# Squared-ReLU MLP: warm-up matmuls as four concurrent column tiles, and the natural-layout weight group kept only in the first block

## The chip, the cores and the metric

The kernel runs on one core of one Trainium2 chip. The metric is device time in microseconds (us) of one execution. A "span" is the time from the first to the last profiled instruction; it is about 1.8 us shorter than the device time of the same execution.

## The reference

```python
# x (1, 2048, 576), w1 (576, 4608), b1 (4608), w2 (4608, 576), b2 (576), all bfloat16
def reference(x, w1, b1, w2, b2):
    h = jnp.einsum("bsd,df->bsf", x, w1) + b1
    r = jnp.where(h > 0, h, 0)
    h = r * r
    return jnp.einsum("bsf,fd->bsd", h, w2) + b2
```

## The kernel before

The 2,048 rows of x are worked through in four blocks of 512. The hidden dimension is cut into 36 "f-tiles" of 128. The contraction of the first product is 576 = 4.5 x 128, an awkward size: nine pieces of 64. The kernel has two ways to deal with it.

- **Row tiles** (32 of the 36 f-tiles): the array is used as two tiles of 64 rows. Each works on its own f-tile, nine matmuls each, and the two run side by side. The weights `w1_h` hold one f-tile's 64-row pieces in the lower half of the partitions and its partner's in the upper half.
- **Natural layout** (the first four f-tiles): four full 128-row matmuls each, and one 64-row piece that is paired with another f-tile's.

The second product runs as full matmuls over 512 output columns, and its remaining 64 columns as two concurrent 64-column tiles (`phase_t`), for two blocks at once.

```python
    WARM = [512] * 6 + [128]
    for i, n in enumerate(WARM):                       # keeps the engine busy until x lands
        keep(nc.tensor.matmul(wps[:, 0:n], lhsT=ones[:, 0:P], rhs=ones[:, 0:n], start=True, stop=True))
    # [...]
    def a_rows(sb, dup_at=None, dup_sb=None):          # row tiles, 16 pairs of f-tiles
        for j in range(NJ):
            # [...]
            for i in range(NC):                        # nine pieces of 64
                keep(nc.tensor.matmul(bx[:], lhsT=w1_h[0:H, LO_C[i], jc], rhs=xT[0:H, LO_W[i], :], ...))
                keep(nc.tensor.matmul(by[:], lhsT=w1_h[H:P, UP_C[i], jc], rhs=xT[H:P, UP_W[i], :], ...))
            evac_h(sb, bx, G + j)
            evac_h(sb, by, G + NJ + j)
    # [...] a_full(sb, order): the natural group, 16 full matmuls and 2 pairs
    for (j0, j1) in [(0, 1), (1, 2), (2, 4), (4, 6), (6, 8), (8, 10), (10, 12)]:
        load_w1(nc.sync, 0, j0, j1)                    # lower half of the partitions
        load_w1(nc.sync, 1, j0, j1)                    # upper half
        # [...]
    load_xT(1)
    for (j0, j1) in [(12, 14), (14, 16)]:
        load_w1(nc.sync, 0, j0, j1)
        load_w1(nc.sync, 1, j0, j1)
    # [...] b2, six loads of w2, further x
    a_full(0, "k_outer")
    a_rows(0, 12, 1)
    a_rows(1)
    a_full(1, "rows_first")
    phase_t(0)
    phase_b(0, hTs[0], dups=(2, 3))
    phase_b(1, hTs[1])
    a_full(2, "g_outer")
    a_rows(2)
    a_rows(3)
    a_full(3, "rows_first")
    phase_t(2)
    # [...]
```

Of the kernel before, what the change touches and what calls it, by code (L numbers as in the profile page):

```python
# [11 lines left out]
BF16 = mybir.dt.bfloat16  # L12
FP32 = mybir.dt.float32
# [4 lines left out]
def kernel(  # L18
# [9 lines left out]
    nc = tc.nc  # L28
    keep = tc.keep_in_program_order
    P = 128  # L30
    H = 64
# [7 lines left out]
    G = 4  # L39
# [18 lines left out]

    wps = ps_o.tile([P, 512], FP32, name="wps", tag="po")
    ones = nc.const_aps.tensor(1.0, [P, 512], BF16)  # L60
    WARM = [512] * 6 + [128]
    for i, n in enumerate(WARM):
        keep(nc.tensor.matmul(wps[:, 0:n], lhsT=ones[:, 0:P], rhs=ones[:, 0:n], start=True, stop=True))  # L63

    xs = const.tile([P, RT, D], BF16, name="x_sb")
    w1n = wpool.tile([P, NK, GW], BF16, name="w1n")
    w1n8 = wpool.tile([P, G // 2, P], BF16, name="w1n8")
    w1_h = wpool.tile([P, NC, FH], BF16, name="w1_h")
    w1_v = w1.rearrange("(c p) f -> p c f", p=H)

    def load_x(eng, rt):
# [9 lines left out]
    def load_w1(eng, h, j0, j1):  # L81
        keep(eng.dma_start(out=w1_h[h * H:(h + 1) * H, :, j0 * P:j1 * P],
                      in_=w1_v[:, :, GW + h * FH + j0 * P:GW + h * FH + j1 * P]))

    load_x(nc.sync, 0)
    load_x(nc.scalar, 1)
# [31 lines left out]
    def dup_windows(sb):  # L118
        xT = xT_blk[sb]
        keep(nc.vector.tensor_copy(out=xT[0:H, SPC:SPC + 4, :], in_=xT[H:P, E3:E3 + 4, :]))  # L120
        keep(nc.vector.tensor_copy(out=xT[H:P, SPC:SPC + 4, :], in_=xT[0:H, O:O + 4, :]))  # L121
# [24 lines left out]
    def x_transpose(j, k):  # L146
        h, q = divmod(j, 2)
        qc = slice(q * P, (q + 1) * P)
        bank, slot, c0 = (half_banks[h][k], 0, k * P) if k < NK else (half_banks[h][2], 1, D - P)
        keep(nc.tensor.transpose(bank[:, slot, qc], xs[:, j, c0:c0 + P], ident[:]))  # L150

    def x_copies(h):
        hc = slice(h * HS, (h + 1) * HS)
        for k in range(NK):
            src = half_banks[h][k][:, 0, :]
            if k % 2 == 0:
                keep(nc.vector.tensor_copy(out=xT0[:, O + k, hc], in_=src))  # L157
            else:
                keep(nc.scalar.copy(out=xT0[:, O + k, hc], in_=src))  # L159
        keep(nc.vector.tensor_copy(out=xT0[:, E3, hc], in_=half_banks[h][2][:, 1, :]))  # L160
# [4 lines left out]
    def make_b1T():  # L165
        b1T_ps = ps_o.tile([P, P], BF16, name="b1T_ps", tag="po")
        keep(nc.tensor.transpose(b1T_ps[:], b1_rows[:], ident[:]))  # L167
        keep(nc.vector.tensor_copy(out=b1T[:], in_=b1T_ps[:, 0:NFT]))
# [6 lines left out]
    def evac_h(sb, bank, ft):  # L175
        r = rpool.tile([P, SB], BF16, name="r", tag="r")
        keep(nc.scalar.activation(out=r[:], in_=bank[:], func=ACT.Relu, bias=b1T[:, ft:ft + 1], scale=1.0))  # L177
        keep(nc.vector.tensor_tensor(out=hTs[sb][:, ft, :], in0=r[:], in1=r[:], op=ALU.mult))  # L178

    def a_rows(sb, dup_at=None, dup_sb=None):  # L180
        xT = xT_blk[sb]
        for j in range(NJ):
            if j == dup_at:
                dup_windows(dup_sb)
            bx = ps_h.tile([P, SB], FP32, name="ph", tag="ph")
            by = ps_h.tile([P, SB], FP32, name="ph", tag="ph")
            jc = slice(j * P, (j + 1) * P)
            for i in range(NC):
                keep(nc.tensor.matmul(bx[:], lhsT=w1_h[0:H, LO_C[i], jc], rhs=xT[0:H, LO_W[i], :],  # L189
                                 start=(i == 0), stop=(i == NC - 1)))  # L190
                keep(nc.tensor.matmul(by[:], lhsT=w1_h[H:P, UP_C[i], jc], rhs=xT[H:P, UP_W[i], :],  # L191
                                 start=(i == 0), stop=(i == NC - 1)))
            evac_h(sb, bx, G + j)
            evac_h(sb, by, G + NJ + j)

    def a_full(sb, order):
        xT = xT_blk[sb]
        banks = []
        for g in range(G):
            pool, tag = (ps_o, "po") if g < 2 else (ps_h, "ph")  # L200
            banks.append(pool.tile([P, SB], FP32, name="pn", tag=tag))

        def pair(i, start, stop):
            keep(nc.tensor.matmul(banks[2 * i][:], lhsT=w1n8[0:H, i, :], rhs=xT[0:H, SPC, :],  # L204
                             start=start, stop=stop, skip_group_check=order == "k_outer"))
            keep(nc.tensor.matmul(banks[2 * i + 1][:], lhsT=w1n8[H:P, i, :], rhs=xT[H:P, E3, :],  # L206
                             start=start, stop=stop, skip_group_check=order == "k_outer"))

        def full(g, k, start, stop):
            keep(nc.tensor.matmul(banks[g][:], lhsT=w1n[:, k, g * P:(g + 1) * P], rhs=xT[:, O + k, :],  # L210
                             start=start, stop=stop))

        if order == "rows_first":
            for i in (1, 0):
                pair(i, True, False)
            for g in (2, 3, 0, 1):
                for k in range(NK):
                    full(g, k, False, k == NK - 1)
                evac_h(sb, banks[g], g)
        else:  # L220
            if order == "k_outer":
                tb_new = [ps_h.tile([P, 2, HS], BF16, name="tb", tag="ph") for _ in range(2)]
                half_banks[1] = tb_new + tb_po

                def part(h, k):
                    hc = slice(h * HS, (h + 1) * HS)
                    for g in range(G):
                        keep(nc.tensor.matmul(banks[g][:, hc], lhsT=w1n[:, k, g * P:(g + 1) * P],  # L228
                                              rhs=xT[:, O + k, hc], start=(h == 0 and k == 0), stop=False,
                                              skip_group_check=True))  # L230

                for j in range(2):
                    for k in range(NK):
                        x_transpose(j, k)
                for j in range(2):
                    x_transpose(j, NK)
                x_copies(0)
                part(0, 0)
                for k in range(NK + 1):
                    x_transpose(2, k)  # L240
                part(0, 1)
                part(0, 2)
                for k in range(NK + 1):
                    x_transpose(3, k)
                x_copies(1)
                dup_windows(0)
                part(0, 3)
                part(1, 0)
                make_b1T()
                for k in range(1, NK):  # L250
                    part(1, k)
            else:
                for g in (2, 3, 0, 1):
                    for k in range(NK):
                        full(g, k, k == 0, False)
            for i in (1, 0):
                pair(i, False, True)
                evac_h(sb, banks[2 * i], 2 * i)
                evac_h(sb, banks[2 * i + 1], 2 * i + 1)

    ft_order = list(range(G))
    for j in range(NJ):
        ft_order += [G + j, G + NJ + j]

    t_order = ft_order[G:] + ft_order[:G]
    EDGES = [0, 384, 512]

    def phase_t(sb):
        pt = ps_o.tile([P, SB], FP32, name="pt", tag="po")
        for i, ft in enumerate(t_order):  # L270
            for h in range(2):
                keep(nc.tensor.matmul(pt[h * DT:(h + 1) * DT, :], lhsT=w2_sb[:, ft, DM:D], rhs=hTs[sb + h][:, ft, :],  # L272
                                      start=(i == 0), stop=(i == NFT - 1)))
        oT = tpool.tile([P, SB], BF16, name="oT", tag="oT")
        keep(nc.scalar.activation(out=oT[:], in_=pt[:], func=ACT.Identity, bias=b2T[:], scale=1.0))  # L275
        ot = tpool.tile([P, RT, P], BF16, name="ot", tag="ot")
        keep(nc.sync.dma_start_transpose(out=ot[:, :, :], in_=oT[:, :]))
        for h in range(2):
            r0 = (sb + h) * SB
            dst = out2[r0:r0 + SB, DM:D].rearrange("(j p) d -> p j d", p=P)  # L280
            keep(nc.sync.dma_start(out=dst, in_=ot[:, :, h * DT:(h + 1) * DT]))
# [20 lines left out]
            load_w1n8(nc.sync, 0)  # L302
            load_w1n8(nc.sync, 1)
    load_xT(1)
    for (j0, j1) in [(12, 14), (14, 16)]:
        load_w1(nc.sync, 0, j0, j1)
        load_w1(nc.sync, 1, j0, j1)
    keep(nc.sync.dma_start(out=b2_bc[:], in_=b2.partition_broadcast(P)))
    for c in (0, 3, 1, 4, 2, 5):
        load_w2(c)  # L310
    load_xT(2)

    alloc_hT(0)
    a_full(0, "k_outer")
    a_rows(0, 12, 1)
    alloc_hT(1)
    load_xT(3)
    a_rows(1)
    a_full(1, "rows_first")
    phase_t(0)  # L320
    phase_b(0, hTs[0], dups=(2, 3))
    phase_b(1, hTs[1])
    alloc_hT(2)
    a_full(2, "g_outer")
    a_rows(2)
    alloc_hT(3)
    a_rows(3)
    a_full(3, "rows_first")
    phase_t(2)
    phase_b(2, hTs[2])  # L330
    phase_b(3, hTs[3], last=True)
# [30 lines left out]
```

## Time and profile before

| | before |
|---|---|
| device time, median of the first 3 runs | 291.73 us |
| span of the profiled run | 289.8 us |
| TensorE busy | 285.1 us (98%) |
| first row pair starts | 9.77 us |
| one slot (row pair, full matmul, or column pair, 512 columns) | 0.216 us |

The kernel is bound by TensorE. The page of the profile says so three times; the lines are its busy table, its chain of work that ended last, and its costliest group.

```profile
PE 285.1 (98%) x2017; PEld 133.7 (46%) x2032; DVE 79.5 (27%) x176; ACT 95.2 (33%) x152; POOL 2.8 (1%) x11
PE 98%; issue 0%; DVE 0%
L191 PE MATMUL ph<-xTw,w_h 64*128 64x512 bf16 x576 | 124.6, 376 | 0.0
```

The last number of the third line is idle time before the group: none. A matmul's mean duration (376 ns) is longer than a slot because consecutive matmuls overlap in the profile; start-to-start times are what count. The next lines are the timeline of TensorE around the end of block 1 (start us, duration us, engine, line, operation, tiles, shape, count).

```profile
72.38 0.38 PE L204 MATMUL pn<-xTw,w1n 64*128 64x512 bf16 x1
72.38 0.38 PE L206 MATMUL pn<-xTw,w1n 64*128 64x512 bf16 x1
72.59 0.38 PE L204 MATMUL pn<-xTw,w1n 64*128 64x512 bf16 x1
72.59 0.38 PE L206 MATMUL pn<-xTw,w1n 64*128 64x512 bf16 x1
73.13 3.40 PE L210 MATMUL pn<-xTw,w1n 128*128 128x512 bf16 x15 [0.16 <-issue]
76.46 7.96 PE L272 MATMUL pt<-hT,w_sb 128*64 128x512 bf16 x72
```

A row pair starts as two lines at the same time. Then comes the natural group (16 matmuls, of which the first is missing from the trace: x15), then the column pairs. Two changes of tiling mode stand here. From the individual starts (in ns: 72,591, then 73,129, with one missing, put 216 earlier) the first takes 0.32 us start to start instead of 0.216; the second 0.31, plus 0.02 in the slot after it.

The last lines are the waits of TensorE, all there are: no matmul waits for a load.

```profile
PE wps L63 <- PEq L346: 0.8, 1, 0.8
PE pn L210 <- issue: 0.3, 2, 0.2
PE po L293 <- issue: 0.3, 2, 0.2
```

### The profile page before, as it was taken

The numbers are of one execution on the slowest core, as the hardware profiler recorded it, in microseconds if no ns is written. First come the engines' busy times: TensorE is split into PE (matmuls) and PEld (weight loads), VectorE is DVE, ScalarE is ACT, GpSimd is POOL, SyncE is SP. The second block draws the span as 40 slices with busy tenths as digits, with TensorE's granted clock in tenths as the row PEclk, the third lists the DMA queues.
The fourth block names the chain that finished last, engine by engine and source line by source line (L and its number), as shares of the span: only waits on it lengthen the run. The fifth ranks groups of instructions, "written<-read, shape, count | busy, mean of one in ns | idle before, by whom it ended". The sixth has DMA issues, their size and how long they took to land.

```text
span 289.8 us, 4679 instructions
## 1 busy us (share of the span) xinstructions
PE 285.1 (98%) x2017; PEld 133.7 (46%) x2032; DVE 79.5 (27%) x176; ACT 95.2 (33%) x152; POOL 2.8 (1%) x11
## 2 busy tenths in 40 slices
PE   8999999999999999999999999999999999999996
PEld 5544444444444444444444444444445444444454
DVE  1644554444502100000025444444440000000001
ACT  2666666666500000000027666666670000000000
POOL 3000000000000000000000000000000000000000
PEclk9999999999999999999999999999999999999999
DMA  7999999400001000000000000000000200000000
GB/s 198 213 235 185 315 388 234 83 0 2 0 19 33 5 20 18 18 18 20 18 18 2 1 2 0 2 0 2 0 2 0 38 18 18 18 20 18 20 18 20
DMA packets 30581, 16.26 MB, mean 56 GB/s; under 512 B 14676, under 2 KB 30560, under 8 KB 30560
## 3 DMA queue, kind: packets, MB, share of 16 engines
q1 hardware_dynamic: 30176, 15.65, 21.7%
q8 instruction: 16, 0.26, 0.4%
q10 hardware_dynamic: 288, 0.30, 0.4%
q14 instruction: 5, 0.04, 0.0%
q0 software_dynamic: 96, 0.01, 0.0%
HBM read 11.36 MB, written 2.36 MB: 47 GB/s over the span
## 4 chain that ended last, share of the span: by engine, by line
PE 98%; issue 0%; DVE 0%
PE po L293 43%; PE ph L189 42%; PE pt L272 5%; PE pn L210 4%; PE pn L228 1%; PE wps L63 1%; PE tb L150 1%; PE ph L191 1%; PE pn L204 1%; DVE o_sb L295 0%; PE b1T_ps L167 0%; PE pn L206 0%
## 5 line engine op out<-in xcount | busy, mean ns | idle before, releaser
L191 PE MATMUL ph<-xTw,w_h 64*128 64x512 bf16 x576 | 124.6, 376 | 0.0
L189 PE MATMUL ph<-xTw,w_h 64*128 64x512 bf16 x576 | 124.6, 376 | 0.0
L293 PE MATMUL po<-w_sb,hT 128*128 128x512 bf16 (+2 forms) x600 | 123.8, 366 | 0.8 <-issue 0.3
L177 ACT ACTIVATE r<-ph,b1T 128x512 bf16<-128x512 f32 x128 | 81.0, 684 | 41.7 <-PE ph L191 41.7
L293 PEld LDWEIGHTS <-hT 128*128 128x128 bf16 x612 | 58.3, 98 | 66.7 <-issue 0.8
L189 PEld LDWEIGHTS <-w_h 64*128 64x128 bf16 x576 | 54.1, 94 | 68.3
L178 DVE TENSOR_TENSOR hT<-r 128x512 bf16<-128x512 bf16 x144 | 61.1, 425 | 75.9 <-ACT r L177 75.4
L191 PEld LDWEIGHTS <-w_h 64*128 64x128 bf16 x576 | 54.1, 94 | 0.0
L295 DVE TENSOR_TENSOR o_sb<-po,b_bc 128x512 bf16<-128x512 f32 (+2 forms) x17 | 11.2, 660 | 125.0 <-PE po L293 125.0
L177 ACT ACTIVATE r<-pn,b1T 128x512 bf16<-128x512 f32 x16 | 10.3, 687 | 68.7 <-PE pn L206 67.4
L272 PE MATMUL pt<-hT,w_sb 128*64 128x512 bf16 x144 | 15.9, 380 | 0.0
L272 PEld LDWEIGHTS <-w_sb 128*64 128x64 bf16 x144 | 8.0, 110 | 7.8 <-issue 0.8
L210 PE MATMUL pn<-xTw,w1n 128*128 128x512 bf16 x45 | 10.4, 379 | 0.4 <-issue 0.3
L210 PEld LDWEIGHTS <-w1n 128*128 128x128 bf16 x48 | 4.5, 98 | 6.0 <-issue 0.8
L275 ACT ACTIVATE oT<-pt,b2T 128x512 bf16<-128x512 f32 x2 | 1.4, 687 | 14.5 <-PE pt L272 14.5
L228 PE MATMUL pn<-xTw,w1n 128*128 128x256 bf16 x32 | 4.8, 304 | 0.0
L228 PEld LDWEIGHTS <-w1n 128*128 128x128 bf16 x32 | 3.4, 110 | 0.6
L63 PE MATMUL wps<-const-bfloat16-1.0 128*128 128x512 bf16 (+1 forms) x7 | 2.8, 581 | 0.8 <-PEq L346 0.8
L157 DVE COPY xTw<-tb 128x256 bf16<-128x256 bf16 x4 | 1.1, 292 | 6.6 <-PE tb L150 6.6
L120 DVE COPY xTw<-xTw 64x2048 bf16<-64x2048 bf16 x4 | 2.8, 690 | 0.2
L121 DVE COPY xTw<-xTw 64x2048 bf16<-64x2048 bf16 x4 | 2.7, 687 | 0.1
L159 ACT COPY xTw<-tb 128x256 bf16<-128x256 bf16 x4 | 1.3, 375 | 3.7 <-PE tb L150 3.7
(23 smaller groups left out, 16.9 us busy)
## 6 DMA issues: line engine op xcount, KB each, us to landing
w_sb<-in_w_dram SPq DMA_DIRECT2D x6, 864.0 KB, 9.6
w_h<-in_w_dram SPq DMA_DIRECT2D x14, 288.0 KB, 6.8
out_dram<-o_sb SPq DMA_DIRECT2D x15, 128.0 KB, 1.7
w_h<-in_w_dram SPq DMA_DIRECT2D x4, 144.0 KB, 3.6
w1n<-in_w_dram SPq DMA_DIRECT2D x4, 128.0 KB, 3.7
x_sb<-in_x_dram ACTq DMA_DIRECT2D x2, 144.0 KB, 2.8
x_sb<-in_x_dram SPq DMA_DIRECT2D x2, 144.0 KB, 3.3
out_dram<-ot SPq DMA_DIRECT2D x4, 64.0 KB, 1.8
```

The costliest lines, as they stand in the source:

```text
L63: keep(nc.tensor.matmul(wps[:, 0:n], lhsT=ones[:, 0:P], rhs=ones[:, 0:n], start=True, stop=True))
L150: keep(nc.tensor.transpose(bank[:, slot, qc], xs[:, j, c0:c0 + P], ident[:]))
L177: keep(nc.scalar.activation(out=r[:], in_=bank[:], func=ACT.Relu, bias=b1T[:, ft:ft + 1], scale=1.0))
L178: keep(nc.vector.tensor_tensor(out=hTs[sb][:, ft, :], in0=r[:], in1=r[:], op=ALU.mult))
L189: keep(nc.tensor.matmul(bx[:], lhsT=w1_h[0:H, LO_C[i], jc], rhs=xT[0:H, LO_W[i], :], start=(i == 0), stop=(i == NC - 1)))
L191: keep(nc.tensor.matmul(by[:], lhsT=w1_h[H:P, UP_C[i], jc], rhs=xT[H:P, UP_W[i], :], start=(i == 0), stop=(i == NC - 1)))
L204: keep(nc.tensor.matmul(banks[2 * i][:], lhsT=w1n8[0:H, i, :], rhs=xT[0:H, SPC, :], start=start, stop=stop, skip_group_check=order == "k_o ...
L210: keep(nc.tensor.matmul(banks[g][:], lhsT=w1n[:, k, g * P:(g + 1) * P], rhs=xT[:, O + k, :], start=start, stop=stop))
L228: keep(nc.tensor.matmul(banks[g][:, hc], lhsT=w1n[:, k, g * P:(g + 1) * P], rhs=xT[:, O + k, hc], start=(h == 0 and k == 0), stop=False, s ...
L272: keep(nc.tensor.matmul(pt[h * DT:(h + 1) * DT, :], lhsT=w2_sb[:, ft, DM:D], rhs=hTs[sb + h][:, ft, :], start=(i == 0), stop=(i == NFT - 1)))
L293: keep(nc.tensor.matmul(po[:, 0:d1 - d0], lhsT=hT[:, ft, jj * P:(jj + 1) * P], rhs=w2_sb[:, ft, d0:d1], start=(i == 0), stop=(i == NFT - 1)))
L295: keep(nc.vector.tensor_tensor(out=o_sb[:, d0:d1], in0=po[:, 0:d1 - d0], in1=b2_bc[:, d0:d1], op=ALU.add))
```

## The change

It does three things: the warm-up's matmuls are cut into four 32-column tiles that run side by side; blocks 1 to 3 treat their first four f-tiles as row tiles too, from a new tile `w1_x` that needs two more loads; and the last two w1 loads of each half are merged into one, which keeps the number of DMAs at 67.

```diff
-    WARM = [512] * 6 + [128]
-    for i, n in enumerate(WARM):
-        keep(nc.tensor.matmul(wps[:, 0:n], lhsT=ones[:, 0:P], rhs=ones[:, 0:n], start=True, stop=True))
+    WARM = [512] * 6 + [64]
+    for n in WARM:
+        for c in range(0, P, 32):
+            keep(nc.tensor.matmul(wps[c:c + 32, 0:n], lhsT=ones[:, 0:32], rhs=ones[:, 0:n], start=True, stop=True))
 [...]
+    w1_x = wpool.tile([P, NC, GW // 2], BF16, name="w1_x")
 [...]
+    def load_w1x(eng, h):
+        keep(eng.dma_start(out=w1_x[h * H:(h + 1) * H, :, :], in_=w1_v[:, :, h * GW // 2:(h + 1) * GW // 2]))
 [...]
-        for j in range(NJ):
-            if j == dup_at:
+        pairs = [] if sb == 0 else [(w1_x, j, j, G // 2 + j) for j in range(G // 2)]
+        pairs += [(w1_h, j, G + j, G + NJ + j) for j in range(NJ)]
+        for n, (w, j, fa, fb) in enumerate(pairs):
+            if n == dup_at:
 [... a_full becomes a_first, for block 0 only; phase_t takes the f-tiles in the order in which they are made ...]
-    for (j0, j1) in [(12, 14), (14, 16)]:
+    for (j0, j1) in [(12, 16)]:
         load_w1(nc.sync, 0, j0, j1)
         load_w1(nc.sync, 1, j0, j1)
+    for h in range(2):
+        load_w1x(nc.sync, h)
 [...]
-    a_full(0, "k_outer")
+    a_first()
     a_rows(0, 12, 1)
 [...]
     a_rows(1)
-    a_full(1, "rows_first")
     phase_t(0)
 [... a_full(2) and a_full(3) go likewise ...]
```

More of the change, by code (lines that the diff above doesn't have):

```diff
@@ L188, in a_rows @@
             for i in range(NC):
-                keep(nc.tensor.matmul(bx[:], lhsT=w1_h[0:H, LO_C[i], jc], rhs=xT[0:H, LO_W[i], :],
+                keep(nc.tensor.matmul(bx[:], lhsT=w[0:H, LO_C[i], jc], rhs=xT[0:H, LO_W[i], :],
                                  start=(i == 0), stop=(i == NC - 1)))
-                keep(nc.tensor.matmul(by[:], lhsT=w1_h[H:P, UP_C[i], jc], rhs=xT[H:P, UP_W[i], :],
+                keep(nc.tensor.matmul(by[:], lhsT=w[H:P, UP_C[i], jc], rhs=xT[H:P, UP_W[i], :],
                                  start=(i == 0), stop=(i == NC - 1)))
-            evac_h(sb, bx, G + j)
@@ L194, in a_rows, with a_first, part @@
-            evac_h(sb, by, G + NJ + j)
-    def a_full(sb, order):
-        xT = xT_blk[sb]
-        banks = []
-        for g in range(G):
-            pool, tag = (ps_o, "po") if g < 2 else (ps_h, "ph")
-            banks.append(pool.tile([P, SB], FP32, name="pn", tag=tag))
-        def pair(i, start, stop):
+            evac_h(sb, bx, fa)
+            evac_h(sb, by, fb)
+    def a_first():
+        xT = xT_blk[0]
+        banks = [ps_o.tile([P, SB], FP32, name="pn", tag="po") for _ in range(2)]
+        banks += [ps_h.tile([P, SB], FP32, name="pn", tag="ph") for _ in range(2)]
+        tb_new = [ps_h.tile([P, 2, HS], BF16, name="tb", tag="ph") for _ in range(2)]
+        half_banks[1] = tb_new + tb_po
+        def part(h, k):
+            hc = slice(h * HS, (h + 1) * HS)
+            for g in range(G):
+                keep(nc.tensor.matmul(banks[g][:, hc], lhsT=w1n[:, k, g * P:(g + 1) * P], rhs=xT[:, O + k, hc],
+                                      start=(h == 0 and k == 0), stop=False, skip_group_check=True))
+        for j in range(2):
+            for k in range(NK):
+                x_transpose(j, k)
+        for j in range(2):
+            x_transpose(j, NK)
+        x_copies(0)
+        part(0, 0)
+        for k in range(NK + 1):
+            x_transpose(2, k)
+        part(0, 1)
+        part(0, 2)
+        for k in range(NK + 1):
+            x_transpose(3, k)
+        x_copies(1)
+        dup_windows(0)
+        part(0, 3)
+        part(1, 0)
+        make_b1T()
+        for k in range(1, NK):
+            part(1, k)
+        for i in (1, 0):
@@ L204, in pair @@
             keep(nc.tensor.matmul(banks[2 * i][:], lhsT=w1n8[0:H, i, :], rhs=xT[0:H, SPC, :],
-                             start=start, stop=stop, skip_group_check=order == "k_outer"))
+                                  start=False, stop=True, skip_group_check=True))
             keep(nc.tensor.matmul(banks[2 * i + 1][:], lhsT=w1n8[H:P, i, :], rhs=xT[H:P, E3, :],
-                             start=start, stop=stop, skip_group_check=order == "k_outer"))
-        def full(g, k, start, stop):
-            keep(nc.tensor.matmul(banks[g][:], lhsT=w1n[:, k, g * P:(g + 1) * P], rhs=xT[:, O + k, :],
-                             start=start, stop=stop))
@@ L213, in a_full @@
-        if order == "rows_first":
-            for i in (1, 0):
-                pair(i, True, False)
-            for g in (2, 3, 0, 1):
-                for k in range(NK):
-                    full(g, k, False, k == NK - 1)
-                evac_h(sb, banks[g], g)
-        else:
-            if order == "k_outer":
-                tb_new = [ps_h.tile([P, 2, HS], BF16, name="tb", tag="ph") for _ in range(2)]
-                half_banks[1] = tb_new + tb_po
-                def part(h, k):
-                    hc = slice(h * HS, (h + 1) * HS)
-                    for g in range(G):
-                        keep(nc.tensor.matmul(banks[g][:, hc], lhsT=w1n[:, k, g * P:(g + 1) * P],
-                                              rhs=xT[:, O + k, hc], start=(h == 0 and k == 0), stop=False,
-                                              skip_group_check=True))
-                for j in range(2):
-                    for k in range(NK):
-                        x_transpose(j, k)
-                for j in range(2):
-                    x_transpose(j, NK)
-                x_copies(0)
-                part(0, 0)
-                for k in range(NK + 1):
-                    x_transpose(2, k)
-                part(0, 1)
-                part(0, 2)
-                for k in range(NK + 1):
-                    x_transpose(3, k)
-                x_copies(1)
-                dup_windows(0)
-                part(0, 3)
-                part(1, 0)
-                make_b1T()
-                for k in range(1, NK):
-                    part(1, k)
-            else:
-                for g in (2, 3, 0, 1):
-                    for k in range(NK):
-                        full(g, k, k == 0, False)
-            for i in (1, 0):
-                pair(i, False, True)
-                evac_h(sb, banks[2 * i], 2 * i)
-                evac_h(sb, banks[2 * i + 1], 2 * i + 1)
@@ L261 @@
+                                  start=False, stop=True, skip_group_check=True))
+            evac_h(0, banks[2 * i], 2 * i)
+            evac_h(0, banks[2 * i + 1], 2 * i + 1)
     ft_order = list(range(G))
@@ L263 @@
         ft_order += [G + j, G + NJ + j]
-    t_order = ft_order[G:] + ft_order[:G]
     EDGES = [0, 384, 512]
@@ L269, in phase_t @@
         pt = ps_o.tile([P, SB], FP32, name="pt", tag="po")
-        for i, ft in enumerate(t_order):
+        for i, ft in enumerate(ft_order):
             for h in range(2):
@@ L323 @@
     alloc_hT(2)
-    a_full(2, "g_outer")
     a_rows(2)
@@ L327 @@
     a_rows(3)
-    a_full(3, "rows_first")
     phase_t(2)
```

## The prediction

> **What bounds the kernel now.** TensorE. The busy table has PE at 285.1 of 289.8 us (98%), the chain that ended last is 98% PE, and no PE wait is over 0.8 us. From the instructions in order of time: a start of 10 us, then equal slots. A pair of 64-row tiles over 512 columns starts every 0.216 us (both within 4 ns); so does a full 128-row matmul, and a pair of 64-column tiles (the 64-wide tail of the second product).
>
> **Natural group into row tiles: no slots saved.** Per block it is 16 full matmuls plus 2 pairs = 18 slots. As row tiles its 4 f-tiles are 2 x 9 pairs = 18 slots: 3.89 us either way, three times. The extra 48 matmuls and weight loads run beside others.
>
> **What goes: two changes of tiling mode.** The Trainium skill, "TensorEngine Tiling (Array Packing)", Key Properties, says that a change of tiling mode drains the engine. The trace agrees: row pair to full matmul 0.32 us start to start instead of 0.216 (correcting for one missing record), full to column pair 0.31 plus 0.02 in the next, column to full 0.32: about 0.11 us each. Blocks 1 and 3 go rows, full, columns; after the change rows, columns. Two drains leave the PE stream: -0.22 us. Block 2 keeps its single change.
>
> **Warm-up.** Seven matmuls, 0.77 to 3.39 us, 427 ns per 512 columns: the slow clock. Four concurrent 32-column tiles should take the same 427 ns per round, and the last round is 64 columns instead of 128: -0.05 us, invisible because the first x tile lands at 3.45 us. One added mode change falls into that gap. The clock rises at 6.65 us, where 256-column matmuls go from 213 to 109 ns. "TensorE: Matmul & The Clock Gate", Part 1, tells of a free-running activity window of about 3.4 us. If column tiles count as more activity, the clock could rise one window earlier, near 3.24 us. But the start is then bound by loads: the landings of w1's first pieces (4.37, 5.69, 6.42, 6.76 us) and of the last x tile (6.04 us); I estimate at most 0.3 us gained, at one chance in three.
>
> **Loads.** The added 0.59 MB is queued behind the last pieces of w1 and before w2. Those pieces are merged into one of 512 columns per half, needed when block 0 reaches its thirteenth pair at 33.5 us. Before, the four pieces landed from 30.5 to 33.6 us; with runs twice as long I expect the merged ones by 32 to 33.5 us: a PE wait of 0 to 0.3 us. The new tile is needed at 41.3 us and should land by 36 us. w2 lands about 1 us later than 47.7 us and is first needed at 76.5 us. The evictions (2 x 0.68 us ACT per 1.94 us pair of f-tiles) keep their margin.
>
> **Predicted: 291.4 us (before 291.73), 8 in 10 between 290.9 and 291.9.** Chances: faster by over 2% 0.005, within 2% 0.98, slower by over 2% 0.015.
>
> **What would show the steps right.** 632 row-pair slots at 0.216 us; rows to columns in one step of about 0.32 us near 76.2 us; warm-up rounds of 427 ns with four starts within about 15 ns; the clock's rise at the same 6.6 us or near 3.2 us.
>
> **What would make it wrong.** Column-tile warm-up matmuls running one after another (24 x 427 ns, +6 us or more); a late merged w1 load; the clock rising a window later.

## The result, and the profile after

| | before | changed |
|---|---|---|
| median of 6 runs each | 291.35 us (291.08 to 291.87) | 292.06 us (291.29 to 292.29) |
| ratio | | 1.0017, 95% interval 0.9999 to 1.0035 |
| span of the profiled run | 289.80 us | 290.51 us |

A ratio is the mean time of one kernel's runs over that of the other's of the same rounds, so it isn't quite the ratio of the medians. I had put the change at -0.33 us and it came out at about +0.5 us by the ratio and +0.7 us by the medians, with an interval that just includes 1, so the sign isn't settled by the timed runs. The two profiled runs differ by 0.71 us, and traces are sharp enough to say where that went.

The page of the changed kernel, the chain that ended last and the two groups that matter:

```profile
PE 87%; SPq 7%; DMA 4%; issue 1%; DVE 0%
L198 PE MATMUL ph<-xTw,w_h 64*128 64x512 bf16 x576 | 125.3, 376 | 0.7 <-DMA w_h<-in_w_dram 0.7
L198 PEld LDWEIGHTS <-w_h 64*128 64x128 bf16 x576 | 54.0, 94 | 33.2 <-DMA w_h<-in_w_dram 1.6
```

The chain was 98% TensorE; now 11% of it is loading and issuing loads, because the chain passes through a load of w1 that was late. TensorE waits for w1 twice. Its timeline around the two waits, the first at the third piece of w1 (columns 2 to 4; columns of w1 are counted in units of 128 here and below), the second at the merged last piece:

```profile
13.61 0.38 PE L196 MATMUL ph<-xTw,w_h 64*128 64x512 bf16 x1
13.61 0.38 PE L198 MATMUL ph<-xTw,w_h 64*128 64x512 bf16 x1
13.82 0.38 PE L196 MATMUL ph<-xTw,w_h 64*128 64x512 bf16 x1
14.44 0.39 PE L198 MATMUL ph<-xTw,w_h 64*128 64x512 bf16 x1 [0.24 <-DMA w_h<-in_w_dram]
14.44 0.39 PE L196 MATMUL ph<-xTw,w_h 64*128 64x512 bf16 x1
...
33.66 0.38 PE L198 MATMUL ph<-xTw,w_h 64*128 64x512 bf16 x1
33.66 0.38 PE L196 MATMUL ph<-xTw,w_h 64*128 64x512 bf16 x1
34.46 0.39 PE L198 MATMUL ph<-xTw,w_h 64*128 64x512 bf16 x1 [0.42 <-DMA w_h<-in_w_dram]
34.46 0.39 PE L196 MATMUL ph<-xTw,w_h 64*128 64x512 bf16 x1
```

Read the starts, not the idle times in brackets. The idle time (0.24 and 0.42 us) is what is left after the previous matmul's 0.38 us have run out; the next slot was due 0.216 us after the previous one. So the delays are 0.617 - 0.216 = 0.40 us and 0.794 - 0.216 = 0.58 us.

There is a third loss that no view of waits shows. At 13.82 us one line stands alone: the lower tile (L196) has its weights and starts, the upper one (L198) does not. From then on, each upper matmul runs beside the *next* lower one. The tiles are out of step by one, and at the end of the rows the last upper matmul runs alone, so that the stream has one slot more. It can be seen at the end of block 1 in the timeline:

```profile
76.77 0.38 PE L198 MATMUL ph<-xTw,w_h 64*128 64x512 bf16 x1
76.77 0.38 PE L196 MATMUL ph<-xTw,w_h 64*128 64x512 bf16 x1
76.99 0.38 PE L198 MATMUL ph<-xTw,w_h 64*128 64x512 bf16 x1
77.29 7.96 PE L254 MATMUL pt<-hT,w_sb 128*64 128x512 bf16 x72
```

L198 at 76.99 has no partner. Rows to column pairs is one step here, 306 ns from start to start (76,986 to 77,292), plus 0.02 in the next slot: one mode change where there were two.

To keep the account clean I split every profiled run into four parts: the start of the first row pair; the *stream*, from there to the last weight load of the program; from the last weight load to the landing of the last output (2.09 us in both kernels, and 2.08 to 2.10 in all); and the *closing*, from that landing to the end.

| profiled run, us | first row pair | stream | closing | span |
|---|---|---|---|---|
| before | 9.773 | 277.030 | 0.91 | 289.80 |
| changed | 9.496 | 278.033 | 0.90 | 290.51 |
| difference | -0.277 | +1.003 | -0.01 | +0.715 |

The stream's +1.003 is: two mode changes fewer, -0.213 (measured below); waits, +0.401 and +0.578; the lone slot, +0.216; and +0.01 for the first slot after each wait (226 ns instead of 216). The sum is 1.002. The earlier first row pair gained nothing by itself: the landing of the late piece sets the restart at 14.44 us, so rows that start 0.28 us earlier only wait that much longer.

The landings explain the waits. The next fence is no view of the profile but a list from the trace's records: landing times in us of the w1 pieces, lower half then upper half, and the start of the first 16,384-byte packet on the instruction queue (the page's "q8 instruction", 16 packets).

```
           columns 1-2     2-4             4-6             last pieces                      first fetch
before     9.02, 10.54     11.90, 13.61    14.97, 16.23    30.48, 31.75, 32.91, 33.60       15.90
changed    9.28, 10.72     12.10, 14.39    15.61, 16.82    31.64, 34.41 (merged)            10.96
```

The merged piece's upper half lands at 34.41 and is needed at 33.88: that is the second wait. The upper half of columns 2 to 4 lands 0.78 us later than before, though nothing in the order of the loads up to there has changed. What has changed is that TensorE has 42 more instructions in its warm-up (28 matmuls and 28 weight loads instead of 7 of each), and that the first fetch of instructions in the run comes 4.9 us earlier, while that piece is in flight.

### The profile page after: what moved, and what is told of

It is laid out like the page before. It is cut to its first block, busy times and chain, and to the rows that moved or that the text cites. A ratio compares the mean times of both kernels' runs of the same rounds, so it can differ in the third digit from the quotient of the medians.

```text
span 290.5 us, 4821 instructions
## 1 busy us (share of the span) xinstructions
PE 285.5 (98%) x2089; PEld 133.8 (46%) x2101; DVE 79.6 (27%) x176; ACT 95.0 (33%) x152; POOL 2.8 (1%) x11
## 4 chain that ended last, share of the span: by engine, by line
PE 87%; SPq 7%; DMA 4%; issue 1%; DVE 0%
PE po L275 43%; PE ph L196 24%; PE ph L198 15%; PE pt L254 5%; SPq L84 5%; DMA w_h<-in_w_dram 3%; SPq L132 2%; DMA x_sb<-in_x_dram 1%; SPq L133 0%; SPq L81 0%; DVE o_sb L277 0%
## 5 line engine op out<-in xcount | busy, mean ns | idle before, releaser
L198 PE MATMUL ph<-xTw,w_h 64*128 64x512 bf16 x576 | 125.3, 376 | 0.7 <-DMA w_h<-in_w_dram 0.7
L196 PE MATMUL ph<-xTw,w_h 64*128 64x512 bf16 x576 | 125.3, 376 | 0.0
L182 ACT ACTIVATE r<-ph,b1T 128x512 bf16<-128x512 f32 x140 | 88.5, 684 | 110.5 <-PE ph L198 87.8
L196 PEld LDWEIGHTS <-w_h 64*128 64x128 bf16 x576 | 54.0, 94 | 36.4
L198 PEld LDWEIGHTS <-w_h 64*128 64x128 bf16 x576 | 54.0, 94 | 33.2 <-DMA w_h<-in_w_dram 1.6
L196 PE MATMUL ph<-xTw,w_x 64*128 64x512 bf16 x54 | 12.1, 376 | 0.0
L198 PE MATMUL ph<-xTw,w_x 64*128 64x512 bf16 x54 | 12.1, 376 | 0.0
L196 PEld LDWEIGHTS <-w_x 64*128 64x128 bf16 x54 | 5.0, 94 | 4.5 <-issue 0.4
L198 PEld LDWEIGHTS <-w_x 64*128 64x128 bf16 x54 | 5.0, 94 | 2.1
L257 ACT ACTIVATE oT<-pt,b2T 128x512 bf16<-128x512 f32 x2 | 1.4, 687 | 13.6 <-PE pt L254 13.6
L64 PE MATMUL wps<-const-bfloat16-1.0 128*32 128x512 bf16 (+1 forms) x28 | 2.8, 575 | 0.8 <-PEq L327 0.8
L213 PEld LDWEIGHTS <-w1n 128*128 128x128 bf16 x32 | 3.3, 106 | 0.4
L182 ACT ACTIVATE r<-pn,b1T 128x512 bf16<-128x512 f32 x4 | 2.4, 688 | 2.1 <-PE pn L239 2.1
L125 DVE COPY xTw<-xTw 64x2048 bf16<-64x2048 bf16 x4 | 2.8, 690 | 0.2
```

The costliest lines, as they stand in the source:

```text
L64: keep(nc.tensor.matmul(wps[c:c + 32, 0:n], lhsT=ones[:, 0:32], rhs=ones[:, 0:n], start=True, stop=True))
L125: keep(nc.vector.tensor_copy(out=xT[0:H, SPC:SPC + 4, :], in_=xT[H:P, E3:E3 + 4, :]))
L182: keep(nc.scalar.activation(out=r[:], in_=bank[:], func=ACT.Relu, bias=b1T[:, ft:ft + 1], scale=1.0))
L196: keep(nc.tensor.matmul(bx[:], lhsT=w[0:H, LO_C[i], jc], rhs=xT[0:H, LO_W[i], :], start=(i == 0), stop=(i == NC - 1)))
L198: keep(nc.tensor.matmul(by[:], lhsT=w[H:P, UP_C[i], jc], rhs=xT[H:P, UP_W[i], :], start=(i == 0), stop=(i == NC - 1)))
L213: keep(nc.tensor.matmul(banks[g][:, hc], lhsT=w1n[:, k, g * P:(g + 1) * P], rhs=xT[:, O + k, hc], start=(h == 0 and k == 0), stop=False, s ...
```

## The experiments

Theory A: the merged load is late, and that is the loss. Rivals: row tiles cost something of their own (B); the column tiles of the warm-up do (D, F). After the first four runs, theory E (the instruction fetch) and theory G (the closing) were added. All eleven experiments gave correct results. The experiments were run in three batches on different chips, each beside runs of the kernel before. Kernels are compared only within the same rounds.

### 1. Changed kernel, last load split again

```diff
-    for (j0, j1) in [(12, 16)]:
+    for (j0, j1) in [(12, 14), (14, 16)]:
```

> The changed kernel with the last w1 load split again into two of 256 columns per half; all else as changed. Theory A (late merged load): the 0.79 us step of the row-pair stream at 33.66 us is gone, the upper half's piece lands by 33.2 us, and the kernel is 0.5 to 0.8 us faster than the changed one (292.06), about 291.3 to 291.5. Rival B (the extra time comes from the early wait at 13.8 us and from the tiles slipping out of step, whatever the last load does): unchanged, 291.9 to 292.3.

Measured: 292.51 us, ratio 1.0043 to before. The late wait is gone, as A said, but the kernel isn't faster; A's number fell. The rival named there, the early wait and the tiles out of step, is what the trace shows (run 2 calls another rival B). There is one gap in the row stream, 1.166 us at 13.87 us, where the upper half of columns 2 to 4 landed at 14.99 us. And the closing took 1.27 us instead of 0.90. So the merged load is a cause of a wait, and not the only loss.

### 2. Only the row tiles

The split as in 1, and the warm-up of before.

> Row tiles in blocks 1 to 3 with the split last load and the full-width warm-up of before: only the row-tile part of the change. Theory A: two mode changes fewer and no late load, so 0.2 us under the kernel before, 0.1 to 0.3. Rival B (row tiles cost something of their own, for instance through the added 0.59 MB): at or above the kernel before.

Measured: 291.65 us, ratio 1.0016 (1.0003 to 1.0028). At first sight B. But the stream is 276.818 us, 0.212 shorter than before: the gain from the mode changes is there, to the size predicted. There is no wait for w1_h. The closing took 1.28 us, 0.37 more than before, and so hides it. This is what gave rise to theory G.

This run also happens to answer for the clock. The timeline of its start:

```profile
3.52 0.73 PE L154 MATMUL tb<-ident,x_sb 128*128 128x128 bf16 x10
4.35 0.60 PE L212 MATMUL pn<-xTw,w1n 128*128 128x256 bf16 x4
4.79 0.44 PE L154 MATMUL tb<-ident,x_sb 128*128 128x128 bf16 x5
5.47 0.61 PE L212 MATMUL pn<-xTw,w1n 128*128 128x256 bf16 x4 [0.24 <-DMA w1n<-in_w_dram]
6.62 0.61 PE L212 MATMUL pn<-xTw,w1n 128*128 128x256 bf16 x4 [0.54 <-DMA w1n<-in_w_dram]
```

The clock was at full speed at 3.5 us (ten transposes in 0.73 us; in before, at the slow clock, 1.25), three microseconds earlier than in before's trace. Yet the first row pair started at 9.68 us against 9.77: TensorE waited for w1's first pieces instead.

### 3. Kernel before, last load merged

```diff
-    for (j0, j1) in [(12, 14), (14, 16)]:
+    for (j0, j1) in [(12, 16)]:
```

> The kernel before with only the last w1 load merged to 512 columns per half. Theory A: the row-pair stream of block 0 waits near 33.5 us for the upper half, 0.5 to 1 us, and the kernel is slower than before by as much. Rival: no wait, same time within 0.1 us.

Measured: 292.14 us, ratio 1.0037. The upper half lands at 33.93 us and is waited for, as A said, though for less than the 0.5 us expected. The timeline:

```profile
33.16 0.38 PE L189 MATMUL ph<-xTw,w_h 64*128 64x512 bf16 x1
33.16 0.38 PE L191 MATMUL ph<-xTw,w_h 64*128 64x512 bf16 x1
33.38 0.38 PE L189 MATMUL ph<-xTw,w_h 64*128 64x512 bf16 x1
33.97 0.39 PE L191 MATMUL ph<-xTw,w_h 64*128 64x512 bf16 x1 [0.22 <-DMA w_h<-in_w_dram]
33.98 0.39 PE L189 MATMUL ph<-xTw,w_h 64*128 64x512 bf16 x1
```

Again the tiles go out of step. The stream is 277.632 us, 0.602 over before: the wait of 0.381 (0.597 - 0.216) and the lone slot of 0.216 make 0.597.

### 4. Kernel before, warm-up as four column tiles

> The kernel before with only the warm-up as four column tiles. Theory C (phase of the clock's window is free): the rise of the clock falls anywhere between about 4 and 7.5 us, the time is that of before within 0.3 us. Rival D (column tiles raise the clock earlier): rise near 6.1 us as in the changed kernel, the rows start 0.28 us earlier, and the third w1 piece (needed at 13.8 us) is waited for, up to 0.6 us.

Measured: 292.03 us, ratio 1.0031. The clock rises after 5.1 us and the start is no earlier (9.80 us), so D's first half is wrong; C's range for the clock holds, its time doesn't; the wait at 14.1 us is there (gap 0.373 us, landing at 14.45), with a first fetch at 11.73 us. The three kernels with the four-tile warm-up so far all have a late third piece (14.39, 14.99, 14.45) and an early fetch (10.96, 11.69, 11.73); the three without it land it by 13.61, 13.13 and 13.18 us and fetch at 15.90, 15.34 and 15.82. Column tiles or fetch: the next run separates them.

### 5. Kernel before, warm-up of 28 full-width matmuls

```diff
-    WARM = [512] * 6 + [128]
+    WARM = [128] * 22 + [64] * 6
```

> The kernel before with its warm-up cut into 28 full-width matmuls (22 of 128 columns, 6 of 64) instead of 7: as long as before (2.67 us at the slow clock), as many instructions as the four-tile warm-up, and no column tiles. Theory E (42 more PE instructions bring PE's first instruction fetch of 16 KB forward from 15.9 to about 11 to 12 us, where it delays the third piece of w1, needed at 14.1 us): fetch at 11 to 12 us, upper half of the third piece lands at 14.3 to 15 us instead of 13.6, the row-pair stream waits 0.2 to 0.9 us there, time 0.3 to 0.9 us over before. Rival F (the column tiles themselves do it): third piece by 13.7 us, no wait, time of before within 0.2 us.

Measured: 291.97 us, ratio 1.0028 (1.0014 to 1.0043). Fetch at 10.97 us, third piece at 14.23 us, and the wait, with no column tile in the warm-up:

```profile
13.37 0.38 PE L189 MATMUL ph<-xTw,w_h 64*128 64x512 bf16 x1
13.38 0.38 PE L191 MATMUL ph<-xTw,w_h 64*128 64x512 bf16 x1
13.59 0.38 PE L189 MATMUL ph<-xTw,w_h 64*128 64x512 bf16 x1
14.28 0.39 PE L191 MATMUL ph<-xTw,w_h 64*128 64x512 bf16 x1 [0.31 <-DMA w_h<-in_w_dram]
14.28 0.39 PE L189 MATMUL ph<-xTw,w_h 64*128 64x512 bf16 x1
```

Without any column tile, 42 more instructions do it. Rival F falls.

### 6. Kernel before, one column-tile round, few instructions

```diff
-    WARM = [512] * 6 + [128]
+    for c in range(0, P, 32):
+        keep(nc.tensor.matmul(wps[c:c + 32, :], lhsT=ones[:, 0:32], rhs=ones[:], start=True, stop=True))
+    WARM = [512] * 5 + [128]
```

> The kernel before with only the first of its six 512-column warm-up matmuls as a round of four column tiles: column tiles are there, but only 6 PE instructions more than before instead of 42. Theory E (instruction fetch): the first fetch comes about 0.3 us earlier than in before, at 15 to 15.6 us; no wait in the row-pair stream; time of before within 0.2 us. Rival F (the column tiles themselves): late third piece and a wait near 14 us, time 0.3 us or more over before.

Measured: 291.53 us, ratio 1.0003 (0.9991 to 1.0016). Fetch at 15.58 us, third piece at 13.05 us, no gap, stream 277.029 us. One round of column tiles by itself costs nothing measurable.

### 7. Kernel before, two loads more

```diff
     def load_w2(c):
-        keep(nc.sync.dma_start(out=w2_sb[:, c * W2CH:(c + 1) * W2CH, :], ...))
+        for f0, f1 in ([(0, 6)] if c not in (2, 5) else [(0, 3), (3, 6)]):
+            a, e = c * W2CH + f0, c * W2CH + f1
+            keep(nc.sync.dma_start(out=w2_sb[:, a:e, :], in_=w2_view[:, a:e, :]))
```

> The kernel before with two of the six w2 loads cut in two: two DMAs more, none of them near a deadline. Theory G (the closing waits on the DMA queues' semaphores go in a fixed order, and with two DMAs more the last output DMA is the first in that order, so six other waits follow it instead of preceding it): the time from the landing of the last DMA to the end is 1.27 us instead of 0.91, time 0.3 to 0.4 us over before. Rival: 0.91 us and the same time within 0.1 us.

Measured: 291.60 us, ratio 1.0012 (1.0000 to 1.0024). The closing took 1.27 us, as G said. The records of SyncE's closing semaphore waits, relative to the landing of the last output, show why:

```
before (67 DMAs)   -1.08 -1.02 -0.96 -0.89 -0.83 -0.77 | 0.02           end 0.91
two DMAs fewer     -1.07 -1.02 -0.95 -0.89 | 0.02 0.07 0.14              end 1.02   (run 3)
two DMAs more      | 0.02 0.07 0.14 0.21 0.27 0.33 0.39                  end 1.27   (run 7)
```

There are seven waits at about 0.06 us apiece, one after the other. The one that the last output holds up is last, fifth or first in the row, depending on the number of DMAs in the program. Those behind it are paid for after the landing.

### 8. and 9. The parts that gain, without those that lose

The row tiles of run 2, with another pair of loads merged to get the number of DMAs back to that of before; these pieces are needed at 25.7 us.

```diff
-    for (j0, j1) in [(0, 1), (1, 2), (2, 4), (4, 6), (6, 8), (8, 10), (10, 12)]:
+    for (j0, j1) in [(0, 1), (1, 2), (2, 4), (4, 6), (6, 8), (8, 12)]:
```

> Row tiles in blocks 1 to 3, the full-width warm-up, the last w1 load split in two as before, and the fifth and sixth of the early pieces merged instead (columns 8 to 12, needed at 25.7 us, landing by about 23.6), so that the number of DMAs is that of before. By theories A, E and G together: no wait in the row-pair stream, fetch near 15.4 us, the short closing (0.91 us), two mode changes fewer: 0.15 to 0.35 us faster than before. If any of them is wrong: at or above before.

> The best version again, beside the other two, since its interval still held 1: 0.15 to 0.35 us faster than before; the PE stream from the first row pair to the last weight load 276.82 us as in the first run of it (277.03 in before).

Measured: 290.92 us, ratio 0.9993 (0.9981 to 1.0005), and again 290.97 us, ratio 0.9986 (0.9972 to 0.9999). Stream 276.817 and 276.818 us, closings 0.89 and 0.91 us. TensorE's waits, all of them, in the second of the two runs, then the head of its chain:

```profile
PE wps L63 <- PEq L326: 0.8, 1, 0.8
...
PE 99%; DVE 0%; issue 0%
```

The stream is settled: 0.212 us shorter. The time is 0.2 to 0.4 us under before by the ratios, of which one interval includes 1 and the other just doesn't. It has the lowest medians.

### 10. The changed kernel, loads re-cut around the early fetch

```diff
-    for (j0, j1) in [(0, 1), (1, 2), (2, 4), (4, 6), (6, 8), (8, 10), (10, 12)]:
+    for (j0, j1) in [(0, 1), (1, 2), (2, 3), (3, 4), (4, 6), (6, 8), (8, 12)]:
-    for (j0, j1) in [(12, 16)]:
+    for (j0, j1) in [(12, 14), (14, 16)]:
-    W2CH = 6                      # and the order of the loads to match
+    W2CH = 9
```

> The changed kernel with its four-tile warm-up kept and the loads re-cut around the early fetch: third piece of w1 in two of 128 columns per half, columns 8 to 12 in one, the last again in two, w2 in four loads instead of six, so that the number of DMAs is that of before. Theories A, E, G: fetch still at 11 to 12 us; the first half of the third piece is needed at 13.8 us and lands near 13.5 to 14.2 us, so the wait shrinks to 0 to 0.4 us (0.6 to 1.2 in the other kernels with that warm-up); short closing of 0.9 us; faster than the changed kernel by 0.4 to 1 us, between 290.9 and 291.7. If the wait stays at 0.6 us or more, the size of the piece is not what sets its landing.

Measured: 291.28 us, ratio 0.9997 (0.9984 to 1.0009). The fetch is still early (11.12 us), and the upper half of columns 2 to 3 still lands 2.8 us after the lower half (13.57 after 10.81), but it is only needed at 14.06 us. The timeline at that place:

```profile
13.62 0.38 PE L196 MATMUL ph<-xTw,w_h 64*128 64x512 bf16 x1
13.63 0.38 PE L198 MATMUL ph<-xTw,w_h 64*128 64x512 bf16 x1
13.84 0.38 PE L196 MATMUL ph<-xTw,w_h 64*128 64x512 bf16 x1
13.84 0.38 PE L198 MATMUL ph<-xTw,w_h 64*128 64x512 bf16 x1
14.06 0.38 PE L196 MATMUL ph<-xTw,w_h 64*128 64x512 bf16 x1
14.06 0.38 PE L198 MATMUL ph<-xTw,w_h 64*128 64x512 bf16 x1
```

The tiles stay in step, and the stream is 276.817 us. With the warm-up of the change kept, all of its loss in the stream can be had back by the loads alone.

### 11. Before, once more

> The kernel before once more, unchanged, for a second trace and the spread: ratio 1 within 0.1%, no wait in the row-pair stream, fetch at 15 to 16 us, closing 0.91 us; the rise of the clock at another time than 6.65 us if the window is free-running.

Measured: 291.25 us, ratio 1.0001 (0.9988 to 1.0014); stream 277.030 us, to the nanosecond that of the first trace; fetch at 15.33 us, closing 0.91 us. The last slow matmul started at 4.2 us, against 6.6 us in the first trace of the same kernel.

### The ledger

| profiled run | first row pair | gaps in the row stream | first fetch | stream | closing |
|---|---|---|---|---|---|
| before | 9.77 | none | 15.90 | 277.030 | 0.91 |
| before_again | 9.59 | none | 15.33 | 277.030 | 0.91 |
| b_tail | 9.43 | none | 14.25 | 277.029 | 1.27 |
| col_few | 9.59 | none | 15.58 | 277.029 | 0.89 |
| b_warm | 9.80 | 0.373 | 11.73 | 277.409 | 0.90 |
| warm28 | 9.26 | 0.690 | 10.97 | 277.726 | 0.89 |
| b_merge | 9.62 | 0.597 | 15.82 | 277.632 | 1.02 |
| changed | 9.50 | 0.617, 0.794 | 10.96 | 278.033 | 0.90 |
| a_split | 9.54 | 1.166 | 11.69 | 277.988 | 1.27 |
| rows_only | 9.68 | none | 15.34 | 276.818 | 1.28 |
| a_fix | 9.73 | none | 11.12 | 276.817 | 0.90 |
| rows_best | 9.68 | none | 15.83 | 276.817 | 0.89 |
| rows_best_2 | 9.55 | none | 16.08 | 276.818 | 0.91 |

The streams without a gap have just two values, 277.03 and 276.82, and their difference is the two mode changes. A first gap adds its whole start-to-start length to the stream, not its length less a slot: the slot in which one tile ran alone is paid again at the end. In b_warm, b_merge and warm28 the stream grew by 0.379, 0.602 and 0.696 us for gaps of 0.373, 0.597 and 0.690. A gap is counted from a run's own start: warm28 has the longer gap partly because its rows started 0.54 us before those of b_warm, and its stream ended earlier (286.99 us against 287.21).

## Why the prediction was right or wrong

**The small gain did not come.** I predicted 291.4 us, -0.33 us. The median was 292.06 us, just outside the 8-in-10 interval, and 0.71 us over the 291.35 us that before had in those six runs.

- **No slots saved: right.** The streams without gaps differ by the mode changes and nothing else.
- **Two mode changes, -0.22 us: right.** Measured -0.212 us, in four runs of three kernels. "TensorEngine Tiling (Array Packing)" of the Trainium skill, Key Properties, states that a change of mode drains the engine; it gives no size, and here it was 0.106 us each.
- **Warm-up invisible: wrong.** Its length was as predicted (2.80 us, against 2.83 for seven full-width matmuls), and the four tiles of the first round start within 10 ns (in later rounds within 30 ns, not the 15 ns I named). What I left out was the count of instructions. 42 more of them bring the first instruction fetch of the run forward to 11.0 to 11.7 us, and the piece of w1 then in flight lands late: columns 2 to 4, which had 0.5 us to spare in before (landed at 13.61, needed at 14.10). The cost in the stream is 0.40 us of waiting plus 0.22 us for the lone slot.
- **The clock: the cap was right, the rest isn't settled.** Over 13 traces the last slow matmul started between 3.3 and 6.6 us: before 6.6 and 4.2, warm-ups of four-tile rounds 5.9, 5.4, 5.1 and 6.4. So no sign that column tiles raise the clock earlier, and the 0.28 us by which the changed kernel's rows started earlier lies within what kernels with a plain warm-up show (9.26 to 9.77 us). This agrees with the free-running window of "TensorE: Matmul & The Clock Gate", Part 1, though no run proves it. That an early rise would be eaten by the loads is what run 2 showed.
- **Loads, "a PE wait of 0 to 0.3 us": mis-sized.** The merged upper half landed at 34.41 us (33.93 alone, in run 3) instead of by 33.5. The wait was 0.58 us in the changed kernel, and 0.38 plus the lone slot in run 3. I had assumed that longer runs would make up for the merging; they did not, and a merged load lands as one: none of it could be used early.
- **Not in the prediction at all: the two tiles out of step,** one slot for the first wait that catches one tile of a pair alone.

**How sure is the fetch?** That 42 early instructions do it is shown: runs 4 and 5 have it, run 6, with 6, hasn't. That the piece is late *because the fetch holds part of the load up* is inferred, on close evidence. In all 13 profiled runs some piece lands 0.7 to 1.7 us late, on a usual spacing of about 1.2 us (in run 10, with smaller pieces, about 2.2 on 0.55), just after the first fetch starts: in before, columns 6 to 8 (17.49, then 19.45), which had time to spare.

The trace also records sixteen completions for each load, and there are 16 DMA engines. Of the late piece's upper half in the changed kernel, fifteen came by 13.28 us and the sixteenth at 14.39; in the piece before it the last two lay 0.06 apart, and in the pieces after it the sixteenth stays about 1.1 behind. The same step of the sixteenth alone, 0.7 to 1.9 us, is in all 13 traces, just after the first fetch starts, whose packet takes 0.9 to 1.3 us. That is what one DMA engine of sixteen, held up once, would look like. The packets carry no engine number, so it isn't shown that the fetch sits on that engine, and I can't forbid the fetch: it was never taken away, only moved.

"Runtime: NRT & Kernel Launch", Instruction fetch mechanics, tells of refills in blocks of 16 KiB, 256 instructions, by a DMA queue that the sequencer drives, and calls the cost of crossing a block "mostly hidden". The trace agrees on the blocks (16 packets of 16,384 bytes; the sixth and seventh fetch of each run lie 247 to 257 recorded matmuls and weight loads apart). By this reading it was hidden wherever the loads had time to spare and wasn't where a piece had about half a microsecond.

**What stays open.** The changed kernel's six runs fall into two groups, 291.29 and 291.35 against 291.96 to 292.29. Perhaps in some executions a wait is escaped; only one has a profile. Nor do I know why 42 instructions, which take 2.3 us at the pace of the row pairs (four per 0.216 us), move the fetch by 4 to 5 us. The first fetch doesn't come at a fixed count: 192 to 204 matmuls and weight loads had started by then in the five runs with the 28-matmul warm-up, 214 to 246 in the other eight, 37 more on average, which take 2.0 us at that pace. What holds the fetch back in those eight wasn't tested.

## What to carry to other kernels

Instructions are traffic too: a change that adds instructions early, even idle ones, moves the fetch of the next 16 KB of program, and here a load with half a microsecond to spare was pushed over its deadline; so check the landings against the times of need, not only the bytes. When two tiles shared the array, a wait that caught only one of them cost its whole gap, because they stayed out of step until the mode changed. And when a profile says that a part should have gained and the time doesn't, split the span into start, stream and closing: the stream repeated within 2 ns between executions here, while start and closing moved by tenths of a microsecond for reasons of their own.

## What the Trainium skill lacked or had wrong

- "Runtime: NRT & Kernel Launch", Instruction fetch mechanics: the cost of a block is called mostly hidden. During heavy loading it seems not to be: an earlier first fetch (11.0 to 11.7 us instead of 14.3 to 16.1) went with a w1 piece landing at 14.2 to 15.0 us instead of 13.1 to 13.6, and a stream longer by 0.38 to 1.17 us in the runs with no other wait. That fetches go with late data loads isn't said there.
- "TensorEngine Tiling (Array Packing)", Key Properties: a change of mode drains, without a size. Here 0.106 us for each change removed between 64-row, 128-row and 64-column tiles at the full clock.
- "TensorE: Matmul & The Clock Gate", Part 3: tile concurrency is described, not what a wait in one tile does. Here the tiles stay one matmul out of step, one slot of 0.216 us more.
- No page has the closing: seven semaphore waits of about 0.06 us in a fixed order, and a closing of 0.90, 1.02 or 1.27 us with 67, 65 or 69 DMAs in the program.
